# Seven-product sums of the last two tiles on VectorE, and a planner that searches the early stretch first

## The chip, the core and the metric

The kernel runs on one core of a Trainium2 chip. A core has TensorE (matrix products into PSUM), VectorE, ScalarE and GpSimd (element-wise work) and SyncE, which issues transfers; each takes its instructions in the order in which they were written. The metric is the device time of one execution in microseconds, as the median of the runs. In the profile TensorE is PE (its weight loads PEld), VectorE DVE, ScalarE ACT, GpSimd POOL, SyncE SP.

## The reference

A linear attention with a decaying state is followed by a dense block whose activation is g = h - tanh(h). All is fp32; the two weight matrices arrive as 64-bit floats and are converted on the chip.

```python
# r, k, v: batch 4, heads 8, 768 steps, 48 wide; w, u: 8 x 48
for t in range(S):
    cur = einsum('bhd,bhe->bhde', u[None] * kt, vt)
    y[:, :, t] = einsum('bhd,bhde->bhe', rt, state + cur)
    state = w[None, :, :, None] * state + einsum('bhd,bhe->bhde', kt, vt)
x = y.transpose(0, 2, 1, 3).reshape(3072, 384)
h = x @ w_in            # w_in 384 x 2048
out = (h - tanh(h)) @ w_out   # w_out 2048 x 384
```

## The kernel before

**Units.** The attention is cut into 24 units: 12 chunks of 64 steps, each in two halves of two batches. A unit n loads r, k and v (two transfers each on SP, line 730), transposes r and k on TensorE (742), scales them (rT on VectorE at 746, kT on ScalarE at 755), multiplies the state and the keys with the queries (levels, 697), masks the result (896), forms rk and du (759, 763, 886) and its diagonal (767), then multiplies with v and adds to the state (outputs and state, 697 and 860, 905). Its result goes to xt (833, 854). A unit needs the state that unit n - 2 left.

**Dense tiles.** Two units make one block j of 256 tokens; there are 12 blocks. A block is worked in eight tiles of 256 of the 2048 columns, f = 0, 2, ... 14. A tile has two halves of h on TensorE (167), five activations on ScalarE (176 to 184), four operations on VectorE (191 to 197, the last one finishes g), and then the product with w_out. That product is done either plainly (two halves `o`, 205) or with seven products in place of eight blocks (255): for it, three sums of parts of g are formed first on GpSimd (240, 242, 244), and combinations of w_out on VectorE (mixed, 264); at the end of the block the results are collected on VectorE (274 to 283). Blocks 0 to 5 are worked in three passes over the columns (4, 4 and 8), the others one after the other. The last block does its first seven tiles with seven products and the last tile plainly.

**Weights.** They come in 16 pieces of 768 KB, w_in and w_out by turns, into four staging buffers. A piece is converted by five operations on VectorE and two on ScalarE (136 to 142).

**Order.** The order of all instructions is made by a planner in the program, `Plan`, while the kernel is built. Each task has an engine, a cost in microseconds and the tasks it needs. `forward` plays the tasks through: each engine takes the ready task with the earliest due time. `backward` turns a plan into latest times, which serve as due times. `order` then tries 1000 random changes of the due times, in windows of random place and width, and keeps those whose plan doesn't end later. Where TensorE would stand idle at the start, `filled` puts in filler matmuls with the identity (632), in two widths. Nothing is reordered on the chip.

Of the kernel before, what the change touches and what calls it, by code (L numbers as in the profile page):

```python
# [33 lines left out]
AHEAD = 2  # L34
# [3 lines left out]
OWN = 1  # L38
SWAP = 2
ALONE = 2  # L40
SEVEN = 8


# [101 lines left out]
class Dense:  # L145
# [88 lines left out]

    def sums_of_g(self, t, x):

        add, g, s = self.nc.gpsimd.tensor_tensor, t.g.rearrange("p (a t) -> p a t", a=4), None
        if x == 0:
            t.s4 = self.seven.pool().tile([128, 4, C], F32, name="sg", tag="sg", bufs=3)
            add(t.s4[:, :2], g[:, 0::3], g[:, 1:2].to_broadcast([128, 2, C]), ALU.add)  # L240
        elif x == 1:
            add(t.s4[:, 2], t.s4[:, 1], g[:, 0], ALU.add)  # L242
        else:
            add(t.s4[:, 3], t.s4[:, 2], g[:, 2], ALU.add)  # L244
# [54 lines left out]
class Plan:  # L299
# [5 lines left out]


    HOP, NEAR_HOP, LANDS, LANDED, LANES, EARLY, SPARE, WARM, SLOW = 0.16, 0.06, 2.4, 1.6, 8, 45.0, 20.0, 6.0, (60.0, 3.0)
    CHUNK, CHUNK_0, ASKED, COMES, FIRST = 256, 192, 55, 3.4, 9.5
    BEGIN = {"PE": 1.5, "DVE": 2.2, "ACT": 1.2, "POOL": 4.3, "SP": 1.2}

# [3 lines left out]
    def add(self, engine, cost, run, after=(), due=1e9, data=0, gated=False, steps=0):  # L314
        t = SimpleNamespace(engine=engine, cost=cost, run=run, after=[x for x in after if x], due=due, data=data,
                            gated=gated, steps=steps, then=[], n=len(self.tasks))
        for x in t.after:
            x.then.append(t)
        self.tasks.append(t)
        return t  # L320
# [9 lines left out]
                waiting[t.engine].append(t)  # L330
        return waiting

    def forward(self, due):

        ready = [max(self.FIRST, due[t.n] - self.EARLY) if t.gated else 0.0 for t in self.tasks]
        count = [len(t.after) for t in self.tasks]
        waiting = self.queues(ready, count)
        free, lanes, channel = dict(self.BEGIN), {}, 0.0
        step, bound, comes, fills = 0, self.CHUNK_0, 0.0, iter(self.fills)
        filling = next(fills, None)  # L340
        starts, done, last, first, changed = [None] * len(ready), [], 0.0, {}, set(waiting)
        self.fitted = []
        while len(done) < len(ready):
            for e in changed:
                ts = waiting[e]
                first.pop(e, None)
                if not ts:
                    continue
                start = max(free.get(e, 0.0), min(ready[x.n] for x in ts))
                t = min((x for x in ts if ready[x.n] <= start + 1e-9), key=lambda x: (due[x.n], x.n))  # L350
                if t.data:
                    start = max(start, lanes.setdefault(e, [0.0] * self.LANES)[0])
                else:

                    soon = [x for x in ts if ready[x.n] < start + t.cost and due[x.n] < due[t.n] - self.SPARE]
                    if soon:
                        t = min(soon, key=lambda x: (ready[x.n], x.n))
                        start = max(start, ready[t.n])
                first[e] = start, t
            e = min(first, key=lambda x: (first[x][0], x))  # L360
            start, t = first[e]
            waiting[e].remove(t)
            changed = {e}
            end = start + t.cost
            if e == "PE":
                if filling:
                    runs = self.filled(filling, free[e], start, starts)
                    self.fitted.append((free[e], t.n, runs))
                    step += 4 * len(runs)
                    if t is filling[1]:  # L370
                        filling = next(fills, None)
                step += t.steps
                if step >= bound:
                    each = t.cost / max(t.steps, 1)
                    crossed = end - (step - bound) * each
                    late = max(0.0, comes - crossed)
                    end += late
                    comes = max(crossed + late + self.ASKED * each + .3, channel) + self.COMES
                    bound += self.CHUNK
            free[e] = end  # L380
            if t.data:
                channel = max(channel, start + 1.2) + t.data
                end = max(end + self.LANDS, channel + self.LANDED) + self.slow(start)
                lanes[e] = lanes[e][1:] + [end]
            starts[t.n] = start
            last = max(last, end)
            done.append(t)
            for x in t.then:
                ready[x.n] = max(ready[x.n], end + self.hop(t, x))
                count[x.n] -= 1  # L390
                if not count[x.n]:
                    waiting[x.engine].append(x)
                    changed.add(x.engine)
        return last, starts, done

    def slow(self, start):
# [42 lines left out]
                    changed.add(x.engine)  # L439
        return latest  # L440

    def order(self, tries=1000):


        due = [t.due for t in self.tasks]
        for t in reversed(self.tasks):
            for x in t.then:
                due[t.n] = min(due[t.n], due[x.n] - t.cost - self.HOP - (self.LANDS if t.data else 0))
        plan = self.forward(due)
        for _ in range(4):  # L450
            due = self.backward(plan)
            plan = self.forward(due)
        chance = Random(5)
        for _ in range(tries):
            by, at, wide = chance.choice((0.3, 1, 2, 5)), chance.uniform(0, plan[0]), chance.choice((15, 40, 100, 700))
            moved = [x + chance.gauss(0, by) * (abs(start - at) < wide / 2) for x, start in zip(due, plan[1])]
            other = self.forward(moved)
            if chance.random() < .5:
                latest = self.backward(other)
                again = self.forward(latest)  # L460
                if again[0] < other[0]:
                    other, moved = again, latest
            if other[0] <= plan[0]:
                plan, due = other, moved
        self.due = due
        _, starts, done = plan
        self.forward(due)
        fitted, order = {n: (free, runs) for free, n, runs in self.fitted}, []
        for t in done:
            t.start = starts[t.n]  # L470
            free, runs = fitted.get(t.n, (0.0, [])) if t.engine == "PE" else (0.0, [])
            order += [SimpleNamespace(engine="PE", cost=0.0, start=free, run=run) for run in runs]
            order.append(t)
        return order
# [19 lines left out]
def near(ctx, tc, r, k, v, w, u, out, shared, moe_w_in, moe_w_out):  # L494
# [4 lines left out]
    d = shared["dims"]  # L499
# [5 lines left out]
    work = ctx.enter_context(tc.tile_pool(name="n_work", bufs=2))  # L505
# [6 lines left out]
    def fixed(name, shape, dt=F32):  # L512
        return const.tile(shape, dt, name=name, tag=name)

    plan = Plan()
    add = plan.add
    e_of = {"SP": Q, "ACT": A, "PE": T, "DVE": V, "POOL": G}
    dense = Dense(nc, work, gpool, ps_d, shared, out,
                  lambda n: [(n % 2 * 2 + z) * d.S + n // 2 * SHORT for z in range(2)], lambda t: new_outs(t), shared["last"])
# [8 lines left out]
    by, plus = (work.tile([128, NP, SHORT + 1], F32, name=x, tag=like) for x, like in (("by", "tg"), ("plus", "q")))  # L528
# [416 lines left out]
    def hidden(j, fs, f, due, pace, seven=False):  # L945
        t = dense.tile(j, fs, f)
        none = SimpleNamespace(g=None, c1=None, c2=None, cp=None, o=None, h=None, s=None, q=None, small=None, th=None, tg=None, empty=[], emptied=[])
        m = len(tiles)
        b1, b2, b3, b5 = (tiles[m - i] if m >= i else none for i in (1, 2, 3, 5))
        x = SimpleNamespace(empty=[], emptied=[])  # L950
# [14 lines left out]
        x.c2 = add("DVE", .6, lambda: dense.vec(t, "c2"), [x.q, x.c1])  # L965
        x.cp = add("DVE", .65, lambda: dense.vec(t, "cp"), [x.c2, x.small, x.g])
        if seven:
            x.sg = add("POOL", .75, lambda: dense.sums_of_g(t, 0), [x.cp, b3.o, b1.cp])
            for i in (1, 2):
                x.sg = add("POOL", .5, lambda i=i: dense.sums_of_g(t, i), [x.sg])  # L970
            done = units[L * (FIRST + 2) - 1]
            now = add("PE", 1.32, lambda: dense.products(t, 0), [x.sg, mixed[f // 4], b1.o, done.cp, done.diag, done.lev] + b1.empty + b1.emptied[:2], due + 2 * pace, steps=16)
            x.o = add("PE", .99, lambda: dense.products(t, 1), [now] + b1.emptied, due + 2 * pace + 1.3, steps=12)
            if t.last:
                finished_seven(t, x, now, due, pace)
            return
# [23 lines left out]
    now, done = 22.0, 0  # L1000
# [9 lines left out]
    for j in range(FIRST, d.NB):  # L1010
        ends = (d.NF,) if j < d.NB - 1 else (d.NF - ALONE, d.NF)
        for at, end in zip((0, *ends), ends):
# [323 lines left out]
```

## Time and profile before

| | us |
|---|---|
| median of 3 runs (604.02 to 606.13) | 604.15 |
| the profiled execution, its own time | 606.31 |
| its span, first to last instruction | 604.5 |
| PE busy | 583.7 (97%) |
| PEld busy | 493.8 (82%) |
| DVE busy | 466.9 (77%) |
| ACT busy | 403.6 (67%) |
| POOL busy | 204.6 (34%) |

The chain of work that ended last lies on PE for 81% of the span, on DVE for 8% and on ACT for 5%. The last matmul ends at 596.3; what follows is one addition on DVE and the last transfers to memory. A row of a view has the start and the length of an instruction or of a group of the same kind, then the engine, the line of the program and the tiles; in brackets stands how long the engine was idle before it and what released it. A fp32 matmul of the program is two records.

### The profile page before, as it was taken

How to read it: one execution, taken by the hardware profiler on the slowest of the kernel's cores; microseconds unless marked ns; L12 is line 12 of the kernel's file. 1: busy time of each engine (PE TensorE's matmuls, PEld its weight loads, DVE VectorE, ACT ScalarE, POOL GpSimd, SP SyncE). 2: the span in 40 equal slices, each digit the busy share in tenths (PEclk: the TensorE clock that was granted, in tenths of full speed). 3: DMA queues.
4: the chain of work that ended last, by engine and by line, in shares of the span. 5: the costliest groups of instructions: out<-in, count | busy, mean ns of one | idle time of the engine just before them, and what ended most of it. 6: DMA issues, size and time to landing. Idle time of an engine off the chain costs nothing.

```text
span 604.5 us, 14282 instructions
## 1 busy us (share of the span) xinstructions
PE 583.7 (97%) x5597; PEld 493.8 (82%) x5597; DVE 466.9 (77%) x775; ACT 403.6 (67%) x902; POOL 204.6 (34%) x372
## 2 busy tenths in 40 slices
PE   7889998999999999999999999999999999999994
PEld 5556776777777689899999999888989988899993
DVE  5789989999999999987667856756986665744753
ACT  3677988899986575656666655757784757665551
POOL 5001222301000244554455443432552434453531
PEclk9989999999999999999999999999999999999998
DMA  6986569572621210111011120131310100100101
GB/s 125 185 160 116 97 120 217 112 159 73 125 60 19 48 28 11 30 26 27 2 27 27 29 44 1 35 57 26 65 25 11 41 1 9 27 7 3 26 2 31
DMA packets 86325, 33.77 MB, mean 56 GB/s; under 512 B 78536, under 2 KB 80680, under 8 KB 86248
## 3 DMA queue, kind: packets, MB, share of 16 engines
q1 hardware_dynamic: 81084, 25.57, 21.5%
q0 software_dynamic: 4992, 6.99, 5.2%
q8 instruction: 46, 0.75, 0.6%
q14 instruction: 31, 0.25, 0.1%
q10 hardware_dynamic: 172, 0.20, 0.1%
HBM read 26.94 MB, written 4.72 MB: 52 GB/s over the span
## 4 chain that ended last, share of the span: by engine, by line
PE 81%; DVE 8%; ACT 5%; issue 2%; SPq 1%; DMA 1%; POOL 0%; ACTq 0%; DVEq 0%; POOLq 0%
PE h L167 38%; PE p L255 25%; PE o L205 9%; PE yk_ps L697 6%; DMA st<-in_moe_w_in_dram 1%; PE x_ps L742 1%; DVE rT L746 1%; SPq L730 1%; ACT kT L755 1%; PE yk_ps L742 1%; DVE tg L193 1%; PE x_ps L697 1%; ACT xt L833 1%; ACT s L176 1%; DVE tg L195 1%
## 5 line engine op out<-in xcount | busy, mean ns | idle before, releaser
L167 PE MATMUL h<-xt,w_in_sb 128*128 128x256 f32 x1152 | 283.8, 383 | 2.9 <-issue 1.6
L167 PEld LDWEIGHTS h<-xt,w_in_sb 128*128 128x128 f32 x1152 | 213.7, 191 | 33.8 <-issue 3.0
L240 POOL TENSOR_TENSOR sg<-g 128x256 f32<-128x256 f32 x71 | 54.8, 772 | 178.4 <-DVE g L197 149.7
L191 DVE TENSOR_TENSOR g<-h,th 128x512 f32<-128x512 f32 x96 | 66.0, 688 | 50.8 <-ACT s L176 24.0
L255 PE MATMUL p<-mixed,sg 128*128 128x192 f32 x426 | 104.1, 326 | 0.2 <-issue 0.2
L193 DVE SCALAR_TENSOR_TENSOR tg<-s,tg 128x512 f32<-128x512 f32 x96 | 69.5, 724 | 30.7 <-ACT tg L180 16.9
L178 ACT ACTIVATE th<-h 128x512 f32<-128x512 f32 x96 | 57.4, 597 | 51.8 <-PE h L167 51.8
L180 ACT ACTIVATE tg<-h 128x512 f32<-128x512 f32 x96 | 57.1, 595 | 42.6 <-PE h L167 42.5
L176 ACT ACTIVATE s<-h 128x512 f32<-128x512 f32 x96 | 57.4, 598 | 41.1 <-PE h L167 40.8
L854 POOL DMA_DIRECT2D xt<-rest x66 | 32.2, 494 | 148.4 <-ACT rest L833 147.6
L255 PEld LDWEIGHTS p<-mixed,sg 128*128 128x128 f32 x426 | 75.0, 190 | 0.4 <-issue 0.4
L197 DVE COPY_PREDICATED g<-small,tg 128x512 f32<-128x512 int32 x96 | 71.7, 747 | 4.5
L255 PE MATMUL p<-w_out_sb,g 128*128 128x192 f32 x284 | 70.7, 331 | 0.1
L195 DVE SCALAR_TENSOR_TENSOR tg<-q,tg 128x512 f32<-128x512 f32 x96 | 67.2, 700 | 4.1 <-DVE tg L193 0.5
L182 ACT ACTIVATE q<-s,m1b 128x512 f32<-128x512 f32 x96 | 69.7, 726 | 0.7
L184 ACT ACTIVATE small<-s,smallb 128x512 f32<-128x512 f32 x96 | 69.5, 724 | 0.4
L205 PE MATMUL o<-w_out_sb,g 128*128 128x384 f32 x192 | 69.6, 488 | 0.0
L255 PEld LDWEIGHTS p<-w_out_sb,g 128*128 128x128 f32 x284 | 52.0, 190 | 7.4 <-DVE e L283 0.5
L767 ACT ACTIVATE at<-same,du 128x64 f32<-128x64 f32 x184 | 48.0, 340 | 6.8 <-DVE du L763 6.4
L205 PEld LDWEIGHTS o<-w_out_sb,g 128*128 128x128 f32 x192 | 35.6, 190 | 15.8 <-DVE part L218 0.3
L244 POOL TENSOR_TENSOR sg<-sg,g 128x128 f32<-128x128 f32 x71 | 40.7, 573 | 5.1
L242 POOL TENSOR_TENSOR sg<-sg,g 128x128 f32<-128x128 f32 x71 | 38.8, 547 | 5.4
(129 smaller groups left out, 695.1 us busy)
## 6 DMA issues: line engine op xcount, KB each, us to landing
st<-in_moe_w_out_dram SPq DMA_DIRECT2D x8, 768.0 KB, 6.9
rt<-in_r_dram SPq DMA_DIRECT2D x48, 96.0 KB, 3.1
vt<-in_v_dram SPq DMA_DIRECT2D x48, 96.0 KB, 3.0
st<-in_moe_w_in_dram SPq DMA_DIRECT2D x16, 288.0 KB, 6.0
kt<-in_k_dram SPq DMA_DIRECT2D x44, 96.0 KB, 3.3
out_dram<-o POOLq DMA_DIRECT2D x44, 96.0 KB, 2.1
st<-in_moe_w_in_dram POOLq DMA_DIRECT2D x16, 96.0 KB, 3.7
xt<-rest POOLq DMA_DIRECT2D x66, 16.0 KB, 2.4
```

The source lines that it names most:

```text
L167: self.nc.tensor.matmul(t.h2[:, z], self.w_in_sb[:, t.f // 2, kk, z * 128 : (z + 1) * 128], self.xts[t.j][:, kk].rearrange("p b t -> p (b ...
L176: A.activation(out, t.h, AF.Square)
L178: A.activation(out, t.h, AF.Tanh)
L180: A.activation(out, t.h, AF.Tanh, scale=G1)
L182: A.activation(out, t.s, AF.Square, bias=self.m1b)
L184: A.activation(out, t.s, AF.Relu, bias=self.smallb, scale=-1.0)
L191: V.tensor_tensor(t.g, t.h, t.th, ALU.subtract)
L193: V.scalar_tensor_tensor(t.tg, t.s, C4, t.tg, ALU.mult, ALU.mult)
L195: V.scalar_tensor_tensor(t.tg, t.q, K1, t.tg, ALU.add, ALU.mult)
L197: V.copy_predicated(t.g, t.small.bitcast(I32), t.tg)
L205: self.nc.tensor.matmul(self.outs[i], t.g2[:, z, i * C : (i + 1) * C], self.w_out_sb[:, t.f + z, :], start=t.first and z == 0, stop=t.last ...
L255: self.nc.tensor.matmul(ps[bank][:, half * n : (half + 1) * n], a, b, start=t.first and half == 0, stop=t.last, skip_group_check=True)
```

## The change

The sums of g of block 11, tiles f = 10 and f = 12, go to VectorE; `LATE = 4` sets the two tiles, and their tasks get other costs. `forward` can stop at a time `until`; a plan that is cut off is rated by that time less the work that TensorE has begun, and less 0.05 of the work of VectorE and ScalarE. `order` first makes 2500 tries on the first 240 us by that measure and then 500 on the whole plan, where there were 1000 on the whole.

```diff
+LATE = 4
...
     def sums_of_g(self, t, x):
-        add, g, s = self.nc.gpsimd.tensor_tensor, t.g.rearrange("p (a t) -> p a t", a=4), None
+        engine = self.nc.vector if t.j == self.d.NB - 1 and t.f >= self.d.NF - ALONE - LATE else self.nc.gpsimd
+        add, g = engine.tensor_tensor, t.g.rearrange("p (a t) -> p a t", a=4)
...
+    AHEAD, BUSY = 0.05, 240.0
...
-    def forward(self, due):
+    def forward(self, due, until=1e9):
...
+            if start > until:
+                break
...
+            work[e] = work.get(e, 0.0) + t.cost
...
+        if len(done) < len(ready):
+            last = until - work["PE"] - self.AHEAD * (work["DVE"] + work["ACT"])
         return last, starts, done
...
-    def order(self, tries=1000):
+    def order(self, first=2500, tries=500):
...
+        def moved():
+            by, at, wide = chance.choice((0.3, 1, 2, 5)), chance.uniform(0, until), chance.choice((15, 40, 100, 700))
+            return [x + chance.gauss(0, by) * (start is not None and abs(start - at) < wide / 2) for x, start in zip(due, plan[1])]
+
+        until = self.BUSY
+        plan = self.forward(due, until)
+        for _ in range(first):
+            new = moved()
+            other = self.forward(new, until)
+            if other[0] <= plan[0]:
+                plan, due = other, new
+        plan = self.forward(due)
+        until = plan[0]
         for _ in range(tries):
...
-            x.sg = add("POOL", .75, lambda: dense.sums_of_g(t, 0), [x.cp, b3.o, b1.cp])
-            for i in (1, 2):
-                x.sg = add("POOL", .5, lambda i=i: dense.sums_of_g(t, i), [x.sg])
+            late = j == d.NB - 1 and f >= d.NF - ALONE - LATE
+            x.sg = x.cp
+            for i, cost in enumerate((.33, .2, .2) if late else (.75, .5, .5)):
+                x.sg = add("DVE" if late else "POOL", cost, lambda i=i: dense.sums_of_g(t, i), [x.sg] + ([] if i else [b3.o, b1.cp]))
```

The instructions themselves are otherwise the same; what differs is their order on each engine, and that the new order has 18 fillers (11 wide, 7 narrow) where the old one has 22 (15 and 7).

More of the change, by code (lines that the diff above doesn't have):

```diff
@@ L341, in forward @@
         starts, done, last, first, changed = [None] * len(ready), [], 0.0, {}, set(waiting)
-        self.fitted = []
+        self.fitted, work = [], {}
         while len(done) < len(ready):
@@ L453, in order @@
         chance = Random(5)
+        def moved():
[10 more added lines that the diff above has]
+        until = plan[0]
         for _ in range(tries):
-            by, at, wide = chance.choice((0.3, 1, 2, 5)), chance.uniform(0, plan[0]), chance.choice((15, 40, 100, 700))
-            moved = [x + chance.gauss(0, by) * (abs(start - at) < wide / 2) for x, start in zip(due, plan[1])]
-            other = self.forward(moved)
+            new = moved()
+            other = self.forward(new)
             if chance.random() < .5:
@@ L461, in order @@
                 if again[0] < other[0]:
-                    other, moved = again, latest
+                    other, new = again, latest
             if other[0] <= plan[0]:
-                plan, due = other, moved
+                plan, due = other, new
         self.due = due
```

## The prediction

> **What bounds the kernel now.** I read first the busy times by stretch (window, then PE busy, PE weight loads, DVE, ACT, POOL, granted PE clock, DMA share, GB/s), and then TensorE's filler matmuls (line 632) alone:
>
> ```profile
> 0.00:60.00 60.00, 51.98 (x847) 34.67 (x847) 45.78 (x85) 35.87 (x100) 12.12 (x43) 0.97 0.78 147
> 60.00:120.00 60.00, 57.56 (x1019) 43.57 (x1019) 55.41 (x96) 53.27 (x145) 15.10 (x31) 1.00 0.71 137
> 120.00:240.00 120.00, 119.37 (x924) 92.28 (x923) 117.19 (x189) 93.02 (x187) 19.63 (x30) 1.00 0.29 65
> 240.00:420.00 180.00, 179.03 (x1303) 164.62 (x1302) 129.83 (x218) 111.02 (x232) 83.59 (x143) 1.00 0.13 29
> 420.00:597.00 177.00, 175.75 (x1510) 158.69 (x1509) 118.67 (x191) 110.42 (x240) 74.15 (x127) 1.00 0.09 19
> ...
> 0.00:20.00 20.00, 10.66 (x21) 4.22 (x21) 1.00 0.78 133
> 20.00:60.00 40.00, 9.89 (x23) 3.96 (x23) 0.96 0.78 154
> ```
>
> TensorE is the bound: it lacks 2.4 us in 60 to 120, 0.6 in 120 to 240, 1.0 in 240 to 420 and 1.3 in the last window (0.7 of it after its last matmul). Its own work is the same in both kernels, so the end moves only by what TensorE loses. Most is lost before 60 us: 60 - 51.98 = 8.0 idle, and 10.66 + 9.89 = 20.6 in fillers, which stand where the planner has no work for TensorE. A third loss is in the timeline of TensorE and in its clock by microsecond:
>
> ```profile
> 25.17 2.83 PE L167 MATMUL h<-xt,w_in_sb 128*128 128x256 f32 x12 [1.31 <-DVE w_in_sb L142]
> ...
> 33.31 2.74 PE L632 MATMUL x_ps<-ident 128*128 128x512 f32 x6
> 38.27 0.69 PE L697 MATMUL yk_ps<-rT,state 48*64 48x64 f32 x32 [2.22 <-DVE state L860]
> 38.79 0.65 PE L697 MATMUL x_ps<-rT,kT 48*64 48x64 f32 x32
> 39.37 4.54 PE L167 MATMUL h<-xt,w_in_sb 128*128 128x256 f32 x12
> 43.84 0.69 PE L697 MATMUL yk_ps<-at,vt 64*64 64x64 f32 x32
> ...
> 40.00:41.00 1.00, 1.00 (x3) 0.80 (x3) 1.00 (x3) 0.00 (x0) 0.00 (x0) 0.50 0.78 152
> ```
>
> Twelve h matmuls, issued in 28 - 25.2 = 2.6 us elsewhere, took 4.47 (39.37 to 43.84): after the 2.22 us gap the clock was 0.50, which cost 1.9.
>
> **Part 1, the last two seven-product tiles (j=11, f=10 and 12).** Six adds leave GpSimd for VectorE. GpSimd's rows are 0.77, 0.55 and 0.57 us. VectorE has no such row; its nearest are the two-input adds of 128x384 (0.55) and 128x192 (0.35), so 0.20 per 192 columns: 0.42 for 128x256 and 0.28 for 128x128, together 0.98 a tile. The tail shows what hides it:
>
> ```profile
> 588.47 0.74 DVE L197 COPY_PREDICATED g<-small,tg 128x512 f32<-128x512 int32 x1
> ...
> 590.32 0.84 DVE L193 SCALAR_TENSOR_TENSOR tg<-s,tg 128x512 f32<-128x512 f32 x1 [1.11 <-ACT s L176]
> ```
>
> For f=12 VectorE stands idle 1.11 us between the select that finishes g and its next operation; for f=10 the hole is 2.5 us (583.85 to 586.35). The adds fit by 0.1 us. In the order of the new kernel the first operation of f=14 waits behind them; without the cover it comes up to 1.0 late, and so do f=14's select and the last eight matmuls. The products of f=12 start at 591.11; the sums would be there at 589.21 + 0.98 = 590.2 instead of 591.5 (GpSimd's last add is recorded to 591.48; spans there are rough, and TensorE shows no gap). So nothing is won either: the order of TensorE's last ten steps is the same in both kernels, back to back. Cost 0; ends -0.3 (a wait too small to be recorded) and +1.0.
>
> Here a rule bears on the change. The Trainium skill (SBUF — State Buffer, Who interferes with whom) says that a VectorE instruction with two SBUF inputs and a GpSimd instruction that reads SBUF block each other for the whole instruction. The trace agrees:
>
> ```profile
> 560.96 0.72 POOL L240 TENSOR_TENSOR sg<-g 128x256 f32<-128x256 f32 x1 [4.78 <-DVE g L197]
> ...
> 560.99 1.25 DVE L193 SCALAR_TENSOR_TENSOR tg<-s,tg 128x512 f32<-128x512 f32 x1 [0.17 <-ACT s L176]
> ```
>
> L193's median is 0.68, so it lost 0.57. By the rule up to three blocked operations a tile would be freed, 6 x 0.57 = 3.4 us of VectorE time; by the rows beside these two tiles only L193 at 590.32 is stretched (0.84), so 0.16. Neither reaches the sum, since TensorE does not wait for VectorE there.
>
> **Part 2, the planner's first search.** Another search with other costs reorders nearly every queue. What the built order shows: TensorE has 18 fillers instead of 22; all four that go are the wide kind. A wide filler is two records; the six at 33.31 took 2.74, so 0.9 each, and 4 x 0.9 = **3.6 us** less filling. But a filler that goes is worth nothing if a wait comes in its place, so I followed the new order by hand from the first weights to unit 6, each queue in its order, with the trace's start-to-start steps: half a tile of h or o 1.30, a unit's levels 1.1, its outputs 1.1, a transpose 0.44; VectorE 0.47 for kw, rk, du and state, 0.60 for rT and masks, 0.48 and 0.87 for a weight piece's conversions; ScalarE 0.87 and 0.48.
>
> On SP the first w_in piece goes out one place later (about 0.5 us at 96 KB and 185 GB/s). VectorE then puts unit 2's rk, kw and rT between the conversions, so the first h starts at 27.6, not 25.17. For that, piece 1 is converted by 34.3 instead of 39.1, and the second tile's h runs before unit 3's levels, not after. The second w_out piece (768 KB) is put ahead of unit 3's r and k, which land at about 33.6 by the moved bytes, not 30; kw of unit 3 is due at 35.4, so it is covered by 1.8. Checkpoints (half-tiles of h and o issued before them):
>
> | TensorE starts | before, trace | after, by hand |
> |---|---|---|
> | h of the second tile | 39.37, 2 | 34.3, 2 |
> | unit 3 levels | 38.27, 2 | 39.4, 4 |
> | unit 3 outputs | 43.84, 4 | 41.9, 4 |
> | unit 4 outputs | 51.58, 4 | 49.9, 6 |
> | unit 5 levels | 57.56, 7 | 54.5, 8 |
> | unit 6 levels | 66.18, 11 | 63.1, 12 |
>
> A half-tile is 1.3, so the lead is 1.9 at unit 3's outputs and 3.1 + 1.3 = **4.4 us** at unit 6. Counted the other way: 3.6 of fillers, plus the half-clock burst of 1.9, minus about 1.2 for waits that are longer: 1.5 before unit 2's outputs (mask at 31.7), 1.0 before the second h, 0.7 before unit 3's levels, 1.9 before the first o (its g is ready at 46.0) = 5.1, against 1.3 + 2.2 + 0.4 = 3.9 in the same places before. Both give about 4.3. From there TensorE is full in both orders, and VectorE is not yet the bound: it was idle 60 - 45.8 = 14 us before 60 and 4.6 in 60 to 120.
>
> **The clock.** Does the half clock come back? The Trainium skill (TensorE: Matmul & The Clock Gate, Part 1) throttles after an idle window of about 3.4 us. Taken alone it leaves my gaps (1.9 at most) free, and the gain is 4.3. The row above is stricter: 2.22 us of gap, with only thin 64-wide matmuls after it, was enough. My waits at 30 to 34 and at 44 to 46 leave TensorE busy for some 40% of a stretch of 3.4 us, like that one. I go by the row: between 0 and 1.9 lost, part of it inside later waits; I take 1.0. That gives 4.3 - 1.0 = **3.3 us**.
>
> **Late stretch.** Whole-plan tries go from 1000 to 500. The 4 us that TensorE loses in 60 to 597 can become less or more; I take no change, ends -1.5 and +2.5.
>
> **Sum.** Span 604.5 - 3.3 = 601.2. The profiled execution's own time is 606.31 (1.8 around the span), the runs' median 604.15; the difference is carried to the median: **600.8 us**.
>
> **Rivals.**
> - *The lead is given back.* VectorE was 97.7% busy in 120 to 240 (117.19), and the new order asks more of it before 260. If VectorE sets the pace there, TensorE waits for g and the lead shrinks to about 1: 603.2. For: that share. Against: TensorE was 99.5% busy beside it.
> - *Slower: loads get in each other's way.* In the new SP order the fifth and sixth weight pieces stand 7 to 18 places earlier, ahead of v, r and k of units 8 to 11, and w_out pieces likewise ahead of units 11 and 12. The trace has one case of TensorE stopping in this stretch (1.52 us of "issue" at 100.2, DMA share over 1.0), and SP held a k load for 2.2 us at 98. If each of these pieces makes a unit late, TensorE, which runs in a fixed order, stops about 1.5 us each time. Three stops (4.5) turn the result to slower; four give 604.15 - 3.3 + 6.0 = 606.9. Against: DMA share falls to 0.29 after 120, and these loads leave a busier stretch.
> - *It doesn't do what it says*: the early search finds nothing. Excluded by the 18 fillers, but the chip may wait where they stood: 604.
>
> **How the numbers follow.** Forecast case 0.60 (598.5 to 602.5), lead given back or not realised 0.27 (602.5 to 604.8), loads 0.13 (above 604.8). About 0.5% (3.0 us) is what a measurement can tell from no change, so faster means under 601.1. Of the forecast case 0.53 lies below that, the rest within; of the loads case 0.08 above 607.2. Range 598.0 to 604.8: it leaves out 0.13 above and some 0.05 below.
>
> **What would show it.** Fewer filler records and the second tile's h near 34 us; unit 6's levels near 63; one or no stretch with a clock of 0.5 before 50; TensorE busy over 57 of 60 us in 60 to 120; the tail from the last h to the end unchanged at 604.5 - 589.2 = 15.3 us. I am wrong if TensorE's gaps before 60 grow by what the fillers lost, or if 60 to 240 lacks more than 5 us.

## The result, and the profile after

The new kernel takes 600.5 us (median of 6 runs, 599.5 to 602.09); the kernel before took 604.2 beside it (604.02 to 606.13). The ratio is 0.9927, with a 95% interval of 0.9911 to 0.9944: 3.4 to 5.4 us less. The predicted time was 600.8.

Busy times by stretch, as shown of before (window, its length, then PE, PEld, DVE, ACT, POOL busy, granted PE clock, DMA share, GB/s), here of the new kernel; the last window ends ahead of the tail:

```profile
0.00:60.00 60.00, 51.49 (x919) 35.90 (x920) 48.85 (x91) 41.75 (x116) 13.45 (x45) 1.00 0.80 152
60.00:120.00 60.00, 57.94 (x960) 42.83 (x958) 53.95 (x94) 50.81 (x138) 14.75 (x30) 1.00 0.85 156
120.00:240.00 120.00, 118.05 (x975) 91.77 (x974) 117.70 (x192) 95.10 (x197) 19.22 (x33) 1.00 0.25 57
240.00:420.00 180.00, 178.89 (x1195) 165.58 (x1194) 128.60 (x217) 106.86 (x218) 85.69 (x139) 1.00 0.12 26
420.00:590.00 170.00, 169.58 (x1541) 154.00 (x1539) 113.31 (x185) 108.47 (x238) 70.56 (x121) 1.00 0.09 20
```

The filler matmuls alone, in the new kernel (same columns, PE and PEld only):

```profile
0.00:20.00 20.00, 11.68 (x24) 4.99 (x24) 1.00 0.80 141
20.00:60.00 40.00, 5.43 (x13) 1.96 (x12) 1.00 0.80 157
```

And TensorE's timeline at the places of the checkpoints (start, length, engine, line, operation):

```profile
34.09 2.83 PE L168 MATMUL h<-xt,w_in_sb 128*128 128x256 f32 x12 [0.89 <-DVE w_in_sb L143]
...
38.87 0.69 PE L719 MATMUL yk_ps<-rT,state 48*64 48x64 f32 x32 [0.22 <-DVE rT L768]
...
41.37 0.69 PE L719 MATMUL yk_ps<-at,vt 64*64 64x64 f32 x32 [0.29 <-DVE at L918]
45.53 1.53 PE L206 MATMUL o<-w_out_sb,g 128*128 128x384 f32 x4 [1.56 <-DVE g L198]
...
63.20 0.69 PE L719 MATMUL yk_ps<-rT,state 48*64 48x64 f32 x32
```

Fillers fell from 20.6 to 17.1 us, and each checkpoint lies within 0.6 us of the chain that was followed by hand (second tile's h 34.1 against 34.3, unit 6's levels 63.2 against 63.1). It looks as if the forecast had come true step by step. It had not: the span fell from 604.5 to 597.7, but TensorE's last matmul moved only from 596.3 to 593.2. Before, then after:

```profile
593.55 2.78 PE L205 MATMUL p<-w_out_sb,g 128*128 128x384 f32 x8
```

```profile
590.35 2.85 PE L206 MATMUL p<-w_out_sb,g 128*128 128x384 f32 x8
```

The other 3.7 us lie behind it, in a tail that was forecast as unchanged.

**The tail.** What SyncE waits for in the last microseconds of the kernel before (instruction, releaser: total us, times, longest; a q behind an engine's name stands for its instruction queue):

```profile
SPq L1331 <- PEq L1331: 4.1, 2, 3.6
SPq L1331 <- DMA out_dram<-last: 2.0, 2, 1.5
```

and of the new kernel:

```profile
SPq L1355 <- DMA out_dram<-last: 1.7, 2, 1.1
SPq L1355 <- PEq L1355: 0.7, 2, 0.5
```

A wait of 3.6 us at the program's closing line is gone. The view names TensorE's queue as its releaser, but TensorE had long been done. From the instructions of that closing line, kernel before (shortest/median/longest in ns, first and last start):

```profile
L1331 POOLq EVENT_SEMAPHORE  x4: 17/17/17, 603.7 to 604.4; - x4
L1331 POOLq DRAIN  x3: 46/107/10365, 593.3 to 604.2; - x3
L1331 SPq DRAIN  x3: 7/7/13, 600.2 to 603.9; - x3
L1331 ACTq DRAIN  x2: 8/258/507, 597.7 to 603.9; - x2
...
L1331 DVEq DRAIN  x2: 10/14/17, 599.7 to 604.0; - x2
```

The same line of the new kernel:

```profile
L1355 POOLq EVENT_SEMAPHORE  x4: 17/17/17, 596.9 to 597.6; - x4
L1355 POOLq DRAIN  x3: 46/107/10365, 579.5 to 597.4; - x3
```

And GpSimd's last instruction of the kernel's own work, before and after:

```profile
590.69 0.79 POOL L244 TENSOR_TENSOR sg<-sg,g 128x128 f32<-128x128 f32 x1
```

```profile
576.90 0.46 POOL L246 TENSOR_TENSOR sg<-sg,g 128x128 f32<-128x128 f32 x1
```

Each engine closes with DRAIN instructions, which belong to the program's end and not to the kernel's work. On four engines the longest takes 0.01 to 0.5 us; GpSimd's first one takes 10.365 us, and it begins about 2 us after GpSimd's last instruction. Before, it ran from 593.3 to 603.7, GpSimd's first closing semaphore instruction came right behind it, and the program ended 0.8 later. The section on the time before names one addition and the last transfers as what follows the last matmul. That is not what set the end: the addition was over at 596.9, and SyncE, having waited for the last transfers, was at its own DRAIN at 600.2. From there to 603.7, 3.5 us, only GpSimd's DRAIN is still running. With the last sums of g moved to VectorE, GpSimd's last instruction ends at 577.4 instead of 591.5, the DRAIN is over at 579.5 + 10.4 = 589.9, before the last matmuls have begun, and the end is set by the last addition and its transfers: 4.5 us behind the last matmul, where it was 8.2.

From here on the theory is: the moved adds save the 3 to 4 us by which GpSimd's DRAIN was late, and the new order saves the small rest. The rival is the prediction's own: the new order saves all of it.

### The profile page after: what moved, and what is told of

It is laid out like the page before. It is cut to its first block, busy times and chain, and to the rows that moved or that the text cites. A ratio compares the mean times of both kernels' runs of the same rounds, so it can differ in the third digit from the quotient of the medians.

```text
span 597.7 us, 14262 instructions
## 1 busy us (share of the span) xinstructions
PE 579.0 (97%) x5589; PEld 491.5 (82%) x5589; DVE 465.6 (78%) x781; ACT 403.0 (67%) x902; POOL 203.7 (34%) x366
## 4 chain that ended last, share of the span: by engine, by line
PE 72%; DVE 14%; ACT 5%; issue 4%; DMA 3%; SPq 2%; DVEq 0%; POOL 0%; ACTq 0%; POOLq 0%
PE h L168 34%; PE p L257 25%; PE o L206 5%; PE yk_ps L719 5%; SPq L752 2%; DVE tg L196 2%; DVE tg L194 1%; DVE g L192 1%; DVE g L198 1%; DMA vt<-in_v_dram 1%; PE yk_ps L764 1%; ACT at L789 1%; DMA kt<-in_k_dram 1%; DVE rT L768 1%; DVE mixed L266 1%
## 5 line engine op out<-in xcount | busy, mean ns | idle before, releaser
L168 PEld LDWEIGHTS h<-xt,w_in_sb 128*128 128x128 f32 x1152 | 212.5, 190 | 32.7 <-DVE g L192 1.4
L242 POOL TENSOR_TENSOR sg<-g 128x256 f32<-128x256 f32 x69 | 53.1, 770 | 171.4 <-DVE g L198 105.3
L198 DVE COPY_PREDICATED g<-small,tg 128x512 f32<-128x512 int32 x96 | 75.6, 787 | 4.0
```

What stands on the lines that cost most here:

```text
L168: self.nc.tensor.matmul(t.h2[:, z], self.w_in_sb[:, t.f // 2, kk, z * 128 : (z + 1) * 128], self.xts[t.j][:, kk].rearrange("p b t -> p (b ...
L198: V.copy_predicated(t.g, t.small.bitcast(I32), t.tg)
```

## The experiments

Ratios are against runs of the kernel before on the same chip, with 95% intervals.

**The kernel before once more** (no edit).

> The old kernel once more, for a second profile of it. Theory: TensorE's gap before unit 3's levels (2.2 us) is there again, with the same order and nearly the same starts, and its own time is 604 to 605. Open: whether the half clock after that gap (1.9 us) and the 3.6 us that SyncE waited for TensorE after the last matmul come again. If either is missing, it is chance of one execution and no part of the difference of the medians.

Measured: 604.84, ratio 1.0009 (0.9998 to 1.0019). Its profiled execution has a span of 602.5, 2.0 less than the profile that the prediction was made from, and TensorE's windows and its timeline show where:

```profile
0.00:60.00 60.00, 52.45 (x918) 35.46 (x919) 47.52 (x88) 37.58 (x106) 12.16 (x43) 1.00 0.77 148
...
120.00:240.00 120.00, 119.29 (x921) 92.13 (x920) 117.09 (x189) 92.03 (x186) 19.06 (x28) 1.00 0.29 64
```

```profile
38.83 2.86 PE L167 MATMUL h<-xt,w_in_sb 128*128 128x256 f32 x12
...
64.21 0.69 PE L697 MATMUL yk_ps<-rT,state 48*64 48x64 f32 x32
```

The twelve h matmuls that took 4.54 at half clock take 2.86 here, and unit 6's levels start at 64.2, not 66.2. So the half clock is no fixed part of the old order; the execution profiled first (606.31) was slower than each of the six timed runs beside the result (up to 606.13). Against this one, the new order's lead at unit 6 is 64.2 - 63.2 + 1.3 (one half-tile more) = 2.3; against the first it is 66.2 - 63.2 + 1.3 = 4.3. SyncE's long wait at the closing line, on the other hand, came again, and with it the tail (602.5 - 594.2 = 8.3):

```profile
SPq L1331 <- PEq L1331: 4.4, 2, 3.9
```

**The new order, sums back on GpSimd.** The plan is that of the new kernel; only the engine of the six adds is the old one.

```diff
-        engine = self.nc.vector if t.j == self.d.NB - 1 and t.f >= self.d.NF - ALONE - LATE else self.nc.gpsimd
+        engine = self.nc.gpsimd
```

> The new order kept for every engine; only the six adds of the last two seven-product tiles are executed on GpSimd again, at their new places. Theory (the adds are hidden on either engine): 600.5, within 0.5. Rival (the adds on VectorE carry part of the gain): at least 1 us slower than the new kernel, 601.5 or more, with a wait of TensorE for sg in the last 20 us.

Measured: 603.41, ratio 0.9976 (0.9964 to 0.9989). The new order alone is worth 0.0024 of 604, or 1.4 us (0.7 to 2.2); the adds that "win nothing" account for the rest. The rival's number came, but not by the rival's wait: in the last 20 us TensorE waits for no sum. The closing line of this kernel has the late DRAIN again:

```profile
L1355 POOLq DRAIN  x3: 46/107/10365, 590.8 to 601.7; - x3
```

Its last matmul ends at 594.9, its span at 602.0: 7.1 behind, not 4.5. (This profile also holds a stop of 2.6 us before a filler, put down to issue, and its last matmul is 1.7 later than in the new kernel; the difference of the medians, 2.9, is about that of the tails, 2.6.)

**Hybrids of the two orders.** The first takes the new order up to the levels of unit 6 and the old one after them, the second the reverse; both with the sums on VectorE.

```diff
...
+        cut = 1 + next(i for i, x in enumerate(one) if getattr(x, "n", None) == self.mark)
+        first = {x.n for x in one[:cut] if hasattr(x, "n")}
+        return one[:cut] + [x for x in two if hasattr(x, "n") and x.n not in first]
```

> The new order up to the levels of unit 6 (63 us), then all that is left in the old order. Theory (the gain is made before 63 us and carried): 599.5 to 601.5. Rival (it is made after 63 us, by the search from 63 to 240 or the shorter one on the whole): 603 to 605.

> The mirror: the old order up to the levels of unit 6 (66 us), then all that is left in the new order. Theory: the lead is missing, 603.5 to 605.5. Rival: 600 to 601.5.

Measured: 602.29, ratio 0.9955 (0.9940 to 0.9971), and 604.59, ratio 1.0011 (0.9997 to 1.0025). The first lies between its two expectations, the second where the theory of an early lead put it. They settle little: near the seam TensorE waits 2.0 us in each (at 67 and at 70 us), where neither half was planned for the other, and both profiles hold stretches of half clock. What they do show is the tail, 5.7 and 4.5 us behind the last matmul; in every kernel with the last sums on VectorE and nothing after them on GpSimd it is 4.5 to 5.8.

**The old order, sums on VectorE.** The counterpart, without a seam: every instruction in the place that the old planner gave it, the six adds on another engine.

```diff
-        add, g, s = self.nc.gpsimd.tensor_tensor, t.g.rearrange("p (a t) -> p a t", a=4), None
+        late = t.j == self.d.NB - 1 and t.f >= self.d.NF - ALONE - 4
+        add, g = (self.nc.vector if late else self.nc.gpsimd).tensor_tensor, t.g.rearrange("p (a t) -> p a t", a=4)
```

> The old order of every task, fillers included; only the six adds of the last two seven-product tiles are executed on VectorE, at their old places. New theory (GpSimd closes with a DRAIN of 10.4 us that starts 2.2 us after its last add and ended last in the old kernel; it ends early once the last adds are gone): TensorE's last matmul ends where it did, near 594, and the span ends 4.5 to 6 us after it instead of 8.3: 600.5 to 602. Rival (the recorded one: the adds are hidden, the gain is the new order's lead): 604, within 0.7.

Measured: 601.08, ratio 0.9941 (0.9925 to 0.9957): 3.6 us of the 4.4 that the ratio of the whole change makes, without any new order. The closing line:

```profile
L1332 POOLq DRAIN  x3: 46/107/10365, 582.1 to 599.1; - x3
```

The DRAIN runs from 582.1 to 592.5. The last matmul ends at 593.5, the span 5.8 us behind it; that this is 1.3 more than in the new kernel lies in the last transfers (SyncE waits 3.0 us for them here, 1.7 there), and whether the order or chance makes it no run shows.

**One small copy on GpSimd.** If the DRAIN sets the end, the smallest late instruction must bring it back. After the select that finishes g of the last tile (f = 14), GpSimd copies one column of it into a tile that nobody reads any more.

```diff
+            if t.j == self.d.NB - 1 and t.f == self.d.NF - 2:
+                self.nc.gpsimd.tensor_copy(t.tg[:, :1], t.g[:, :1])
```

> The new kernel with one instruction more: GpSimd copies one column of the last tile's g (f=14) as soon as it is there, near 590.1. New theory: GpSimd's DRAIN then starts near 592.7 and ends near 603, so the span is 603.5 to 604.5 and the time 605 to 606.5, with TensorE's last matmul still ending near 593 to 595. Rival (GpSimd's end is covered by the last transfers, or the DRAIN waits for the amount of GpSimd's work): 600.5, within 0.7.

Measured: 607.29, ratio 1.0045 (1.0033 to 1.0057), slower than both kernels. GpSimd's timeline, then SyncE's waits, then the closing line:

```profile
591.40 0.19 POOL L200 COPY tg<-g 128x1 f32<-128x1 f32 x1 [12.77 <-DVE g L198]
```

```profile
SPq L1357 <- PEq L1357: 6.7, 2, 6.2
SPq L1357 <- DMA out_dram<-last: 2.0, 2, 1.5
```

```profile
L1357 POOLq DRAIN  x3: 46/107/10365, 594.1 to 605.0; - x3
```

A copy of 0.19 us that nobody waits for costs 607.29 - 600.5 = 6.8 us. The last matmul ends at 594.5; the DRAIN ends at 604.4, and the program 0.8 later. The time is 0.8 us above the forecast of 605 to 606.5: here the last tile's g came at 591.3 and not at 590.1, and the DRAIN started 2.5 us after the copy.

**Only the last tile's sums on VectorE** (f = 12; f = 10 back on GpSimd).

```diff
-        engine = self.nc.vector if t.j == self.d.NB - 1 and t.f >= self.d.NF - ALONE - LATE else self.nc.gpsimd
+        engine = self.nc.vector if t.j == self.d.NB - 1 and t.f >= self.d.NF - ALONE - 2 else self.nc.gpsimd
```

> The new order; only the sums of f=12 on VectorE, those of f=10 on GpSimd again. New theory: GpSimd's last add ends near 583, its DRAIN near 595.5, still before the last transfers have landed: 600.5, within 0.7, so one tile would have been enough. Rival (each tile moved brings its share of the 2.9 us that the two brought): 601.5 to 602.5.

Measured: 601.09, ratio 0.9939 (0.9927 to 0.9951), not told apart from the whole change. GpSimd is done at 584.0, the DRAIN at 596.5, with the end at 599.7: one tile is enough.

**Both parts planned anew, one at a time.** In the experiments above the order was held fixed. Here the planner makes its own: first with the new sums and costs and the old search, then with the old sums and the new search.

```diff
-    def order(self, first=2500, tries=500):
+    def order(self, tries=1000):
...
-        until = self.BUSY
-        plan = self.forward(due, until)
-        for _ in range(first):
```

> LATE stays 4 (sums of f=10 and f=12 on VectorE, with the new costs), but the planner searches as before (1000 tries on the whole plan). It arrives at a third order, with 22 fillers as before. If the closing DRAIN of GpSimd decides: its last sum is over by about 580, the DRAIN by about 592, so the end follows the last matmul by 4.5 to 5.7 us as in the other kernels of this kind, and the time is 600 to 602.5. If the early search is what brings the gain: 603.5 to 605.

```diff
-LATE = 4
+LATE = 0
```

> LATE = 0 (sums stay on GpSimd, with the old costs), and the planner searches as in the new kernel; another order again, with 21 fillers. If the closing DRAIN decides: GpSimd's last sum ends near 589, the DRAIN near 602, the last matmul 7 to 8 us before the end, and the time is 602.5 to 605. If the early search brings the gain: 600 to 602.

Measured: 606.68, ratio 1.0017 (0.9988 to 1.0045), and 605.46, ratio 1.0012 (0.9999 to 1.0026). The first misses what the DRAIN theory expected by 4.2 us, the second by 0.5. The first one's tail is as foreseen (DRAIN from 588.0 to 598.3, 4.8 us from the last matmul to the end), but its last matmul ends only at 601.0. The longest waits of its TensorE:

```profile
PE yk_ps L705 <- DVE at L904: 3.6, 4, 1.6
PE h L640 <- issue: 2.9, 1, 2.9
PE yk_ps L705 <- DVE state L868: 2.8, 5, 1.0
```

and its fillers:

```profile
0.00:20.00 20.00, 10.59 (x21) 4.42 (x21) 1.00 0.80 135
20.00:60.00 40.00, 12.37 (x23) 4.55 (x23) 0.92 0.65 134
```

Before 60 us TensorE does 49.4 - 23.0 = 26.4 us of its own work here, 52.4 - 20.7 = 31.7 in the second profile of before, and 51.5 - 17.1 = 34.4 in the new kernel. The search arrived at a poor early stretch. Two stretches of half clock (23 to 26.5 and 57 to 60.5) add to it, but don't explain it alone: the runs with a mean clock of 0.995 or more took 603.12 to 605.79, still above the expected 602.5. The expectation's error was to take the planner as steady: altered costs give another plan altogether. The second kernel has the late DRAIN (593.3 to 603.7, the end at 604.5) and a last matmul at 597.3, 3.1 later than in the second profile of before. With the old costs the early search brought nothing; with the new ones it is 5 to 6 us better than the old search (0.0090 of 604 by the ratios, 6.2 by the medians). Two draws don't say whether it is the better search.

**A longer search** (6000 and 1500 tries), as a candidate to beat both.

```diff
-    def order(self, first=2500, tries=500):
+    def order(self, first=6000, tries=1500):
```

> The new kernel with 6000 and 1500 tries in place of 2500 and 500. If the time is set by TensorE's losses before its last matmul once the DRAIN is out of the way, a plan with fewer of them gives 598.5 to 600; if what the planner counts is smaller than what the chip adds by waits it does not model, 600 to 601.5, no different from the new kernel.

Measured: 601.73, ratio 0.9946 (0.9927 to 0.9965), 0.2 above the second of the two ranges. More tries don't give a faster kernel: DRAIN out of the way at 593.5, tail 4.6, but TensorE does only 49.6 - 20.2 = 29.4 us of its own work before 60, and the last matmul ends at 596.8. Its profile holds two stretches of half clock (25.5 to 28.5 and 52.5 to 56). What the planner counts and what the chip adds by its own waits seem to differ by more than such a search can win; this one run doesn't show it.

**The late fillers left out.**

```diff
+WARMING = 20.0
...
-            order += [SimpleNamespace(engine="PE", cost=0.0, start=free, run=run) for run in runs]
+            order += [SimpleNamespace(engine="PE", cost=0.0, start=free, run=run) for run in runs if free < WARMING]
```

> The new kernel with the fillers after 20 us left out (the other instructions and their order unchanged). If the fillers only stand in idle time: 600.0 to 601.0. If they keep the clock up, each half clock stretch costs 1.7 us, and there would be one or two more in most executions: 602 to 604. If they delay work: under 600.

Measured: 600.71, ratio 0.9934 (0.9911 to 0.9958), like the new kernel. But the clock did fall. Its timeline of TensorE, and then its windows by microsecond:

```profile
22.27 0.68 PE L720 MATMUL yk_ps<-vt,kw 64*64 64x48 f32 x32
24.74 0.66 PE L765 MATMUL x_ps<-ident,kw 128*128 128x128 f32 x4 [1.79 <-DVE kw L894]
27.23 1.13 PE L720 MATMUL yk_ps<-rT,state 48*64 48x64 f32 x32 [1.83 <-DVE rT L769]
28.11 1.10 PE L720 MATMUL x_ps<-rT,kT 48*64 48x64 f32 x32
29.14 4.59 PE L169 MATMUL h<-xt,w_in_sb 128*128 128x256 f32 x12
```

```profile
25.00:26.00 1.00, 0.40 (x4) 0.16 (x2) 1.00 (x3) 0.51 (x2) 0.00 (x0) 0.93 1.03 143
26.00:27.00 1.00, 0.00 (x0) 0.00 (x0) 1.00 (x3) 1.00 (x6) 0.00 (x0) 0.50 1.04 285
...
44.00:45.00 1.00, 1.00 (x12) 0.91 (x8) 1.00 (x3) 0.98 (x4) 0.00 (x0) 0.50 0.83 155
```

Without the fillers the clock halves twice, at 26 to 32.7 and 43 to 46.3. Both stretches overlap waits that stand there anyway, and at unit 6's levels (64.35) only 1.1 us is lost, net of what the missing fillers may have won; that is also the delay of the last matmul (594.3 against 593.2). The median shows 0.2 of it, within the scatter.

## Why the prediction came out, and where it was wrong

The time was right by luck: two errors cancel, each of about 2 to 4 us.

**Part 1: "Cost 0; ends -0.3 ... and +1.0", "So nothing is won either". This step failed.** The old order with the moved adds gains 3.6 us (2.6 to 4.5), the new order loses 3.0 without them. The working beside TensorE was sound: the adds took 0.42, 0.29 and 0.29, forecast as 0.42, 0.28 and 0.28:

```profile
584.81 0.42 DVE L242 TENSOR_TENSOR sg<-g 128x256 f32<-128x256 f32 x1
585.27 0.29 DVE L244 TENSOR_TENSOR sg<-sg,g 128x128 f32<-128x128 f32 x1
585.60 0.29 DVE L246 TENSOR_TENSOR sg<-sg,g 128x128 f32<-128x128 f32 x1
587.34 0.69 DVE L194 SCALAR_TENSOR_TENSOR tg<-s,tg 128x512 f32<-128x512 f32 x1 [1.45 <-ACT tg L181]
```

The cover held too: VectorE still waits 1.45 us after them, and the operation behind the wait takes 0.69 where it took 0.84 beside GpSimd's add, the 0.16 that the prediction had seen. What was missing is the engine that the work leaves. The step asked who waits for the sums, and not what is queued behind them on GpSimd. Behind them stood the DRAIN, and the trace of before had it. The shared SBUF port (the Trainium skill, SBUF — State Buffer, Who interferes with whom), over which a VectorE instruction with two SBUF inputs and GpSimd's reads contend, was rightly given no part in the sum: no run needs it, and moving only f = 12 gives the same time as moving both tiles.

**The tail: "unchanged at 604.5 - 589.2 = 15.3 us". Wrong.** It is 597.7 - 585.7 = 12.0 in the new kernel, and 602.5 - 587.0 = 15.5 in the second profile of before. This was a sign that the prediction itself had named, and the one that showed the error.

**Part 2, the chain to unit 6: right.** Every checkpoint came within 0.6 us, the fillers fell by 3.4 (forecast 3.6), and the waits were where they were put (1.56 before the first o, forecast 1.9). One sum in it is wrong: 28 - 25.2 is 2.8 and not 2.6. The next matmul after the twelve starts at 27.84, so they took 27.84 - 25.17 = 2.67, and the half clock cost 4.47 - 2.67 = 1.8.

**Part 2, its worth: "3.3 us". Mis-sized; it is about 0.8 to 1.4.** (0.8 is the difference of the ratios of the whole change and of the old order with the sums moved, 0.0014 of 604; their intervals overlap, so it isn't told apart from nothing. 1.4 is the new order with the old sums.) Two terms were off. Of the lead of 4.4, 66.2 - 64.2 = 2.0 belonged to the execution profiled first, most of it the half clock: 2.3 is left against the second profile. And "from there TensorE is full in both orders" was wrong: in 120 to 240 the new kernel lacks 120 - 118.05 = 1.95 us, before 0.7. That takes 1.2 of the lead, and the last matmul ends only 594.2 - 593.2 = 1.0 us sooner (0.3 against the old order with the sums moved, 593.5). The rival "the lead is given back" named this place, VectorE as the one waited for, and this size (a lead of about 1, 603.2); the new order with the old sums took 603.41.

**The clock.** Of the rule (the Trainium skill, TensorE: Matmul & The Clock Gate, Part 1: an idle window of about 3.4 us throttles) and the stricter row, the row was the one to go by: without the late fillers, gaps of 1.79 and 1.83 with 0.66 us of matmul between them were enough. Nor is the row a fixed limit: in the second profile of before the gap in its place was 1.84 us, and the clock stayed. The price of 1.0 can't be told by itself: the profiled execution of the new kernel had no half clock, while its runs go from 599.5 at a mean clock of 0.999 to 602.09 at 0.993.

**The median.** The profiled execution's 606.31 was carried to the median as if it were merely offset. It was slower than each timed run beside it, with a disturbance in it that the sum then counted as a saving.

**The loads.** In the new kernel TensorE's waits from 120 to 240 are two, for VectorE (1.4 and 0.6 us), and from 60 to 120 it was busy for 57.9 us; the earlier weight pieces brought no stop, and that rival is out.

## What to carry to other kernels

When work leaves an engine, look at what stands behind it in that engine's own queue up to the program's end, the closing instructions included, which no busy row counts. Here, by the durations in these traces, GpSimd had to be done about 2.2 + 10.4 + 0.8 - 4.6 = 8.8 us before the last matmul ended, or it set the time. Take a second profile before a saving is read from a disturbance (a half clock, a stall) of the first, and test a planner's change with the order held fixed and with the order made anew: the first tells the mechanism, the second how much of the result was the draw.

## What the runs showed of the hardware

- GpSimd's longest closing DRAIN takes 10,365 ns in each of the 13 profiles, whether a sum or the small copy stood before it. It starts 1.8 to 2.5 us after GpSimd's last instruction, and where it ended last (before twice, the new order with the old sums, the one copy, the early search alone) the program ended 0.8 us after it. Why it takes so long stays open.
- The half clock comes and goes between executions of one kernel with the same instructions: twelve h matmuls in 4.54 us in one profile of before, in 2.86 in the next.
- A half clock can cost little where TensorE waits anyway: with the late fillers left out, two stretches, some 10 us in all, came with a last matmul only 1.1 us later.
